# Attention with beacons and a two-layer MLP on one core: the first eight head pairs put in another order

## The chip, the cores and the metric

The kernel runs on one core of one Trainium2 chip. The metric is the time of one execution on the device in microseconds (us), the median over runs. Each core has five engines that run side by side, each with its own queue of instructions: PE (matrix multiply; PEld is its weight load), DVE (vector), ACT (scalar functions), POOL and SP. They wait for each other by semaphores. DMA transfers are issued from the queues of SP, ACT and POOL and move over 16 shared DMA engines.

## What is computed

Causal attention for B = 8 batches, H = 8 heads, S = 576 rows of D = 64, with Nb = 16 "beacon" keys and values that every row sees, and then a two-layer MLP without gate on the 4608 rows of 512:

```python
k_all = np.concatenate([beacon_k, k], axis=2)
v_all = np.concatenate([beacon_v, v], axis=2)
scores = scale * np.matmul(q, k_all.transpose(0, 1, 3, 2))
scores = np.where(causal, -1000000000.0, scores)      # beacons are never masked
a = np.exp(scores - scores.max(-1, keepdims=True))
a /= a.sum(-1, keepdims=True) + 1e-09
x = np.matmul(a, v_all)                               # -> [4608, 512]
h = x @ w_in                                          # [512, 2048]
out = np.maximum(0.01 * h, h) @ w_out                 # [2048, 512]
```

Inputs and output are fp32; the kernel multiplies in bf16 and sums in fp32.

## The kernel before, in words

**Pairs.** Two heads make a pair; pair g = 4 x batch + head pair, 32 in all. Scores are kept transposed (keys on partitions), so that the exponentials are the weights of the second product.

- `score(g, n)` (L286), four parts n = 0..3 of a pair: matmuls of K against Q into one of two PSUM buffers "sc" (L297), then an exp on ACT into the buffer aT (L306). Part n+2 can only start when the exp of part n has freed its buffer. The scores' maximum is not subtracted.
- `masks(g)` (L310): four affine selects on POOL (L320) put zeros where the diagonal blocks are masked.
- `value(g, half)` (L332): aT against V with a column of ones, so the row sums come along (L351); DVE takes the reciprocal (L360) and multiplies (L361) into x_nat. Half 0 has 12 matmuls, half 1 has 18.
- `finish(g)` (L526) calls `x_transposes(g)` (L368): five transposes on PE, one copy on DVE into xT (L378), the MLP's input.

**Q and K.** DMAs issued by POOL bring them in as bf16, two heads of q or k each (L135). For batches 0 and 1, `t_q(g, which)` (L228) transposes them on PE (36 small matmuls a pair, L247) and copies them from PSUM on DVE or ACT (L250); the 16 beacon columns of K are copied on DVE (L238). For batches 2 to 7 POOL permutes them (`permute`, L164), a transposing DMA issued by SP turns them (`turn_pairs`, L262), and POOL puts them in order (`in_order`, L269: L275, L277). K has two buffers (L98), Q two, the raw loads three. The first pair's q and k come in as fp32 by SP and ACT (L152) and are cast on DVE and ACT (L471, L472).

**V** comes in as fp32 by SP (`load_v`, L206), six DMAs a batch, and POOL casts it (`cast_v`, L224), five casts a batch.

**The MLP** works in chunks of 512 rows, 9 in all. Its unit is a *group* of four matmuls of 128x512: `moe1` (L382) makes one of 16 column blocks of the first layer (L387) with the leaky ReLU on ACT (L394); `moe2` (L398) does a quarter of one of four output tiles of the second (L409), after four of which DVE copies the tile (L418) and SP stores it (L420). `fill()` (L425) puts the next group into PE's stream, first and second layer in turn where both can run. A chunk's first layer can start when `finish` has made its rows. There are 288 groups.

**Order.** The order of each engine's queue is written out by hand. Pairs 0 to 7 are in L538 to L562, with three groups among pairs 6 and 7; then a block of its own (L564 to L588) ends pairs 5 to 7 and does 27 more groups before pair 8's first score, so that 30 are done there. From pair 8 on, the groups are spread evenly over eight slots of each pair (L591 to L626). POOL's queue holds in one line all of this: the loads of q, k, w_in and w_out (`loads`, L482), the casts of V, the masks, the permutes and the putting in order. A load issued by POOL waits until the eighth load before it in that queue has landed, as one semaphore serves every eighth.

34 dummy matmuls on the identity stand at the start (`warm_up`, L440).

## Time and profile before

| what | value |
|---|---|
| median of 7 runs | 356.78 us (355.19 to 358.25) |
| time of the profiled execution | 356.68 us |
| span of the profiled execution | 354.9 us |
| PE busy | 340.9 us (96%) |
| POOL busy | 202.0 us (57%) |
| ACT busy | 189.2 us (53%) |
| DVE busy | 94.5 us (27%) |
| first-layer matmuls (L387) | 576, 140.2 us |
| second-layer matmuls (L409) | 592, 139.6 us |
| DMA moved | 40.87 MB, mean 115 GB/s |

The span runs from the first to the last recorded instruction, the time also holds what lies around it. Busy times of an engine count overlapping matmuls once. The profile has a page with the span in 40 slices (a digit is a busy share in tenths), groups of instructions by line, and the chain of work that ended last; the trace gives a time line, with what ended each wait in brackets, and busy times by stretch.

### The profile page before, as it was taken

How to read it: one execution, taken by the hardware profiler on the slowest of the kernel's cores; microseconds unless marked ns; L12 is line 12 of the kernel's file. 1: busy time of each engine (PE TensorE's matmuls, PEld its weight loads, DVE VectorE, ACT ScalarE, POOL GpSimd, SP SyncE). 2: the span in 40 equal slices, each digit the busy share in tenths (PEclk: the TensorE clock that was granted, in tenths of full speed). 3: DMA queues.
4: the chain of work that ended last, by engine and by line, in shares of the span. 5: the costliest groups of instructions: out<-in, count | busy, mean ns of one | idle time of the engine just before them, and what ended most of it. 6: DMA issues, size and time to landing. Idle time of an engine off the chain costs nothing.

```text
span 354.9 us, 7340 instructions
## 1 busy us (share of the span) xinstructions
PE 340.9 (96%) x3002; PEld 172.8 (49%) x3002; DVE 94.5 (27%) x231; ACT 189.2 (53%) x278; POOL 202.0 (57%) x343
## 2 busy tenths in 40 slices
PE   5888999999899999999999999999999999999996
PEld 5566554444454444444444445444444554444444
DVE  2387530102233223221232223222222241000111
ACT  3959754476455873378337843686358403633300
POOL 7599927399899899957695769574441100000000
PEclk9579999999999999999999999999999999999999
DMA  8999999997796986992589355900110011000012
GB/s 163 205 204 167 196 202 195 222 201 128 168 193 118 171 149 120 151 218 36 97 148 223 57 98 119 172 2 1 61 59 2 0 62 59 2 30 30 31 59 88
DMA packets 86929, 40.87 MB, mean 115 GB/s; under 512 B 69872, under 2 KB 82160, under 8 KB 86896
## 3 DMA queue, kind: packets, MB, share of 16 engines
q1 hardware_dynamic: 73456, 26.75, 34.8%
q0 software_dynamic: 13152, 13.34, 24.5%
q10 hardware_dynamic: 288, 0.33, 0.4%
q8 instruction: 23, 0.38, 0.4%
q14 instruction: 10, 0.08, 0.1%
HBM read 37.22 MB, written 9.44 MB: 131 GB/s over the span
## 4 chain that ended last, share of the span: by engine, by line
PE 75%; DMA 9%; POOL 8%; DVE 3%; ACT 2%; issue 2%; SPq 1%; POOLq 0%; ACTq 0%
PE acc L409 32%; PE acc L387 27%; PE sc L297 7%; PE av L351 7%; DMA w_out_sb<-in_moe_w_out_dram 4%; DMA q_raw<-in_q_dram 2%; POOL aT L320 2%; PE tp L373 2%; DMA v_raw<-in_v_dram 1%; DMA v_raw<-in_k_dram 1%; POOL kT L277 1%; POOL qT L277 1%; ACT aT L306 1%; DVE osb L418 1%; PE tp L247 1%
## 5 line engine op out<-in xcount | busy, mean ns | idle before, releaser
L387 PE MATMUL acc<-xT,w_in_sb 128*128 128x512 bf16 x576 | 140.2, 379 | 1.4 <-DVE xT L378 1.4
L409 PE MATMUL acc<-w_out_sb,gT 128*128 128x512 bf16 (+1 forms) x592 | 139.6, 373 | 0.0
L306 ACT ACTIVATE aT<-sc 128x1024 bf16<-128x1024 f32 (+3 forms) x128 | 104.3, 869 | 64.7 <-PE sc L297 64.5
L394 ACT ACTIVATE gT<-acc 128x512 bf16<-128x512 f32 x144 | 85.9, 601 | 79.2 <-PE acc L387 79.2
L409 PEld LDWEIGHTS <-gT 128*128 128x128 bf16 x592 | 53.3, 98 | 58.7 <-issue 6.1
L320 POOL TENSOR_SCALAR_AFFINE_SELECT aT<-aT 128x384 bf16<-128x384 bf16 (+2 forms) x128 | 52.6, 450 | 50.1 <-PE av L351 40.2
L387 PEld LDWEIGHTS <-w_in_sb 128*128 128x128 bf16 x576 | 51.9, 98 | 59.5 <-issue 4.2
L418 DVE COPY osb<-acc 128x512 f32<-128x512 f32 (+1 forms) x37 | 25.1, 677 | 134.7 <-PE acc L409 134.6
L351 PEld LDWEIGHTS <-aT 128*128 128x128 bf16 (+1 forms) x960 | 37.5, 99 | 14.7 <-issue 2.8
L297 PE MATMUL sc<-qT,kT 64*128 64x80 bf16 (+4 forms) x384 | 37.0, 296 | 5.2 <-ACT aT L306 1.6
L351 PE MATMUL av<-v_aug,aT 128*128 128x65 bf16 (+1 forms) x960 | 40.7, 196 | 0.0
L361 DVE TENSOR_TENSOR x_nat<-av,rec 128x384 bf16<-128x384 f32 x64 | 31.4, 491 | 2.2
L224 POOL CAST v_aug<-v_raw 128x512 bf16<-128x512 f32 (+1 forms) x40 | 23.2, 620 | 9.6 <-DMA v_raw<-in_v_dram 9.6
L277 POOL COPY qT<-q_turn 128x576 bf16<-128x576 bf16 x24 | 28.2, 1174 | 0.0
L277 POOL COPY kT<-k_turn 128x576 bf16<-128x576 bf16 x24 | 28.0, 1168 | 0.0
L378 DVE COPY xT<-tp 128x576 bf16<-128x576 bf16 x32 | 14.5, 454 | 49.8 <-PE tp L373 49.8
L297 PEld LDWEIGHTS <-kT 64*128 64x128 bf16 x384 | 12.7, 96 | 30.7 <-issue 18.2
L360 DVE RECIPROCAL rec<-av 128x6 f32<-128x6 f32 x64 | 11.9, 187 | 58.7 <-PE av L351 58.7
L135 POOL DMA_DIRECT2D k_raw<-in_k_dram x31 | 19.3, 624 | 4.2 <-DMA w_out_sb<-in_moe_w_out_dram 4.2
L135 POOL DMA_DIRECT2D q_raw<-in_q_dram x31 | 19.0, 613 | 2.9 <-DMA w_out_sb<-in_moe_w_out_dram 2.8
L164 POOL COPY q_nat<-q_raw 128x1152 bf16<-128x1152 bf16 x12 | 13.8, 1147 | 5.9 <-DMA q_raw<-in_q_dram 5.9
L373 PEld LDWEIGHTS <-x_nat 128*128 128x128 bf16 (+2 forms) x160 | 11.2, 98 | 9.6 <-DVE x_nat L361 1.9
(36 smaller groups left out, 87.6 us busy)
## 6 DMA issues: line engine op xcount, KB each, us to landing
out_dram<-osb SPq DMA_DIRECT2D x35, 256.0 KB, 2.2
v_raw<-in_v_dram SPq DMA_DIRECT2D x24, 256.0 KB, 5.2
q_raw<-in_q_dram POOLq DMA_DIRECT2D x31, 144.0 KB, 4.7
k_raw<-in_k_dram POOLq DMA_DIRECT2D x31, 144.0 KB, 5.2
w_in_sb<-in_moe_w_in_dram POOLq DMA_DIRECT2D x4, 512.0 KB, 6.8
w_out_sb<-in_moe_w_out_dram POOLq DMA_DIRECT2D x4, 512.0 KB, 12.9
v_raw<-in_v_dram SPq DMA_DIRECT2D x8, 224.0 KB, 3.8
v_raw<-in_v_dram SPq DMA_DIRECT2D x8, 160.0 KB, 5.1
```

The costliest lines, as they stand in the source:

```text
L135: dma = nc.gpsimd.dma_start(out=dst[e * RP : (e + 1) * RP], in_=src[b, h0 : h0 + 2].rearrange("h (p i) d -> p h i d", i=RI),)
L224: eng.tensor_copy(out=dst[0 : ROWS[c], c, :, 0:D], in_=t[0 : ROWS[c], c])
L277: nc.gpsimd.tensor_copy(out=dst.rearrange("c (p i) -> c p i", i=RI), in_=t[:, :, e].rearrange("c i p -> c p i"),)
L297: nc.tensor.matmul(out=sc[:, par, col - c0 : col - c0 + w], lhsT=kT[ps_, c * 128 : (c + 1) * 128], rhs=qT[ps_, q0 : q0 + w], start=True, s ...
L306: nc.scalar.activation(out=aT[:, :, c0 : c0 + w], in_=sc[:, :, 0:w], func=AF.Exp, scale=0.125)
L320: nc.gpsimd.affine_select(out=part, in_=part, compare_op=ALU.is_ge, fill=0.0, base=base, channel_multiplier=-1, pattern=pattern,)
L351: nc.tensor.matmul(out=avv[:, n, 0 : D + 1], lhsT=aT[0 : ROWS[c], par, a0 : a0 + 128], rhs=va[0 : ROWS[c], c, 2 * hp + par, :], start=(c = ...
L361: nc.vector.tensor_tensor(out=x_nat[:, t0:t1].rearrange("p t e d -> p (t e) d"), in0=avv[:, :, 0:D], in1=rec[:, n0:n1, None].to_broadcast( ...
L387: nc.tensor.matmul(out=acc, lhsT=w_in_sb[:, j, fc * 128 : (fc + 1) * 128], rhs=xT[:, j, i * 512 : (i + 1) * 512], start=(j == 0), stop=(j ...
L394: nc.scalar.activation(out=gT[i][:, fc, :], in_=acc, func=AF.Prelu, alpha=0.01)
L409: nc.tensor.matmul(out=acc[:, 0:w], lhsT=gT[i][:, fc, t * 128 : (t + 1) * 128], rhs=w_out_sb[:, fc, c0 : c0 + w], start=(fc == 0), stop=(f ...
L418: nc.vector.tensor_copy(out=osb[:, 0:w], in_=acc[:, 0:w])
```

## The change

What it does, by place:

- **Start.** The beacons of batches 0 and 1 are loaded first (by ACT); those of batches 2 to 7 move from the start to pair 7, on POOL. 24 dummy matmuls, the two batches' beacon transposes, 18 dummies, then the transposes of pair 0's Q and K with 4 and 3 dummies behind them. The cast of the first k is split over ACT and DVE, and the copy of the first K into two halves.
- **K has three buffers.** The beacon columns of pairs 2 to 7 are written by POOL, some pairs ahead; all copies of K from PSUM but the first are on DVE.
- **Pairs 0 and 1** have 14 dummy matmuls each among their scores, and their masks are three multiplications by a triangle of ones on DVE (`masks_by_tri`) instead of selects on POOL.
- **Loads.** w_in and w_out come in two halves each instead of four quarters. The first half of w_in is issued during pair 1, behind the Q and K of pairs 4 and 5 and ahead of those of pairs 6 and 7; its second half and w_out's first during pair 6, w_out's second after the masks of pair 7.
- **Pairs 6 and 7.** Eight groups stand at and in pair 6 and five in pair 7, where pairs 5 to 7 are also finished; 17 more follow before pair 8. The second layer starts after 26 first-layer groups instead of 16.
- **From pair 8 on**, POOL puts Q and K in order two pairs ahead (behind the scores of a pair) instead of one; pairs 8 and 9 are done before the cast of batch 2's V; Q and K of batch 3 are loaded before it too; the permutes and loads of the next batch stand behind a pair's masks.

The diff, cut to its core:

```diff
-    k_bufs = [singles.tile([128, NKB * 128], BF16, name=f"kT{i}") for i in range(2)]
+    k_bufs = [singles.tile([128, NKB * 128], BF16, name=f"kT{i}") for i in range(3)]
...
+    def load_w_in(half):
+        cols = slice(half * DF // 2, (half + 1) * DF // 2)
+        return nc.gpsimd.dma_start(out=w_in_sb[:, :, cols], in_=w_in_r[:, :, cols])
+
+    def load_w_out(half):
+        rows = slice(half * NF // 2, (half + 1) * NF // 2)
+        return nc.gpsimd.dma_start(out=w_out_sb[:, rows, :], in_=w_out_r[:, rows, :])
...
-        load_beacon_k(0, 1, nc.scalar)
+        load_beacon_k(0, 2, nc.scalar)
...
+    def beacon_columns(g, eng):
+        b, hp = divmod(g, NPAIR)
+        eng.tensor_copy(out=k_bufs[g % 3][:, 0:NB], in_=bkT[:, b, hp])
...
+        parts = 2 if g == 0 and which == 1 else 1
+        for part in range(parts):
+            p = slice(part * RP // parts, (part + 1) * RP // parts)
+            copy(
+                out=dst.rearrange("c (p i) -> c p i", i=RI)[:, p],
+                in_=ps[:, 0:S].rearrange("c (i p) -> c p i", i=RI)[:, p],
+            )
...
+    def make_tri():
+
+        nc.gpsimd.memset(tri, 1.0)
+        nc.gpsimd.affine_select(
...
+    def masks_by_tri(g):
+
+        aT = probs[g]
+        diag = aT[:, :, 512 : 512 + 3 * 464].rearrange("p e (c x) -> p e c x", c=3)[:, :, :, 0:128]
+        for part, seen in (
+            (aT[:, :, 0:112], tri[:, None, NB:128].to_broadcast([128, 2, 112])),
+            (diag, tri[:, None, None, :].to_broadcast([128, 2, 3, 128])),
+            (aT[0:80, :, 1648:1728], tri[0:80, None, 0:80].to_broadcast([80, 2, 80])),
+        ):
+            nc.vector.tensor_tensor(out=part, in0=part, in1=seen, op=ALU.mult)
...
-        can2 = i2 < NCH and i2 < i1
+        can2 = i2 < NCH and i2 < i1 and done1[0] >= NF + 10
...
+    def keep_busy(n):
+
+        if not busy:
+            busy.append(ps_one.tile([128, 512], FP32, name="av", tag="one"))
         for i in range(n):
-            nc.tensor.matmul(out=ps[:, 0:128], lhsT=ident, rhs=ident, start=True, stop=True)
+            nc.tensor.matmul(out=busy[0][:, 0:128], lhsT=ident, rhs=ident, start=True, stop=True)
...
-        load_beacon_k(1, B, nc.sync)
         load_v(0, after=first)
         load_v(1)
         make_pads()
+        cast_beacon_k(0, 2, nc.scalar.copy)
+        keep_busy(24)
+        beacon_transposes(0, 2)
+        beacon_columns(0, nc.vector)
+        beacon_columns(1, nc.vector)
+        nc.vector.tensor_copy(out=first_cast[0], in_=first_raw[0])
+        nc.scalar.copy(out=first_cast[1][:, 0], in_=first_raw[1][:, 0])
+        nc.vector.tensor_copy(out=first_cast[1][:, 1], in_=first_raw[1][:, 1])
+        keep_busy(18)
+        t_q(0, 0)
+        keep_busy(4)
+        t_q(0, 1, nc.scalar.copy)
+        keep_busy(3)
+        make_tri()
         make_ones()
...
+        beacon_columns(2, nc.gpsimd)
+        cast_v(0, nc.gpsimd, 0, 2)
+        load_qk(1, 0, (0,))
 
         def loads(g):
             b, hp = divmod(g, NPAIR)
             if g == 1:
-                cast_v(0, nc.gpsimd, 3, 5)
+                beacon_columns(3, nc.gpsimd)
+                cast_v(0, nc.gpsimd, 2, 5)
+                load_qk(1, 0, (1,))
+                load_w_in(0)
             elif g == 2:
-                load_qk(1, 1)
+                beacon_columns(4, nc.gpsimd)
             elif g == 3:
-                cast_v(1, nc.gpsimd, 0, 3)
-                load_w_in(0)
+                load_qk(1, 1, (0,))
+                beacon_columns(5, nc.gpsimd)
             elif g == 4:
-                cast_v(1, nc.gpsimd, 3, 5)
-                load_w_in(1)
-                load_w_in(2)
+                load_qk(1, 1, (1,))
+                beacon_columns(6, nc.gpsimd)
             elif g == 5:
-                load_w_in(3)
-                load_w_out(0)
-                load_w_out(1)
...
+                beacon_columns(7, nc.gpsimd)
+            elif g > 2 * NPAIR and b < B - 1:
+                if hp == 0:
+                    load_v(b + 1)
+                    load_qk(b + 1, 0)
+                elif hp > 1:
+                    turn_pairs(b + 1, hp - 2)
...
+            if g < 6:
 
                 score(g, 0)
                 score(g, 1)
...
+                if g < 5:
+                    t_q(g + 1, 0)
+                    t_q(g + 1, 1)
+                    if g in (1, 2):
+                        masks_by_tri(g - 1)
+                if g >= 3:
+                    value(g - 2, 0)
+                if g < 2:
+                    keep_busy(3)
+                score(g, 2)
+                if g < 2:
+                    keep_busy(7)
+                score(g, 3)
+                if g < 2:
+                    keep_busy(4)
+                if g == 2:
+                    value(g - 2, 0)
+                if g >= 2:
+                    value(g - 2, 1)
+                if g >= 3:
+                    finish(g - 3)
+                if g > 1:
+                    masks(g)
+                continue
+
+            if g == 6:
+
+                finish(3)
+                for n in range(4):
                     fill()
+                t_q(6, 0)
+                t_q(6, 1)
+                fill()
+                score(6, 0)
+                score(6, 1)
+                fill()
+                score(6, 2)
+                score(6, 3)
+                cast_v(1, nc.gpsimd, 0, 3)
+                load_w_in(1)
+                cast_v(1, nc.gpsimd, 3, 5)
+                load_w_out(0)
+                masks(6)
+                t_q(7, 0)
+                t_q(7, 1)
+                fill()
+                fill()
+                value(4, 0)
+                value(4, 1)
                 continue
 
+            if g == 7:
+                score(7, 0)
+                score(7, 1)
+                value(5, 0)
+                finish(4)
+                score(7, 2)
+                score(7, 3)
+                masks(7)
+                load_w_out(1)
+                load_beacon_k(2, B, nc.gpsimd)
+                load_qk(2, 0)
+                value(5, 1)
+                value(6, 0)
+                finish(5)
+                value(6, 1)
+                fill()
+                fill()
+                value(7, 0)
+                finish(6)
+                fill()
+                value(7, 1)
+                fill()
+                fill()
+                finish(7)
+                continue
 
+            if g == 8:
                 load_qk(2, 1)
+                cast_beacon_k(2, B, nc.gpsimd.tensor_copy)
                 for grp in range(2):
                     for which in range(2):
                         permute(2, grp, which)
                     turn_pairs(2, grp)
                 load_v(2)
+                while done1[0] + done2[0] < 22:
+                    fill()
+                beacon_transposes(2, B)
+                while done1[0] + done2[0] < 30:
+                    fill()
+                in_order(8)
+                in_order(9)
+                load_qk(3, 0)
                 cast_v(2, nc.gpsimd)
+                load_v(3)
...
             if has(g):
                 score(g, 2)
                 score(g, 3)
+                if has(g + 2):
+                    in_order(g + 2)
...
             if has(g):
                 masks(g)
+                loads_after(g)
```

`loads_after(g)` holds the permutes, the second half of Q and K and the V cast for the next batch that stood in `loads` before. The new dummies' tile takes one of the four PSUM buffers that transposes, values and groups share.

## Prediction

> **What bounds the kernel now.** I read the 40 slices first, then the busy times by stage, the time line, and the chain of waits.
>
> ```profile
> PE   5888999999899999999999999999999999999996
> PEclk9579999999999999999999999999999999999999
> DMA  8999999997796986992589355900110011000012
> ```
>
> PE is full from the fourth slice to the end; losses can only lie in the first 100 us or so. The tail is untouched by the change. Steady state: one chunk's groups and four pairs take 37.32 us (a first-layer run starts at 188.29 and the next at 225.61). A group of four matmuls takes 0.863 us (12 in 2.59), 32 make 27.6, so a pair costs PE (37.32-27.6)/4 = 2.42 us. Pairs 0 to 7 also have Q and K transposed on PE, 0.76 each (27.16 to 27.92).
>
> Up to pair 8 PE should need 8x2.42 + 7x0.76 + 8 groups (6.9) = 31.6 us from the first score (8.55) to the last transpose of pair 7 (49.66), which is 41.1: 9.5 us lost. From there 22 groups run without a gap (19.0) to the first score of pair 8 at **68.59**, with 30 groups done. What follows loses some 2 us: 351.43-68.59 = 282.8 against 24x2.42 + 258x0.863 = 280.7.
>
> ```profile
> 8.00:9.00 1.00, 0.45 (x4) 0.11 (x4) 0.00 (x0) 0.51 (x2) 0.76 (x1) 1.00 1.22 203
> 9.00:10.00 1.00, 1.00 (x37) 0.93 (x36) 0.20 (x1) 1.00 (x2) 0.00 (x0) 0.53 1.19 198
> ...
> 21.00:22.00 1.00, 1.00 (x8) 0.32 (x5) 0.67 (x3) 0.53 (x1) 1.00 (x4) 0.50 1.35 218
> ```
>
> Columns: stretch, length, PE, PEld, DVE, ACT, POOL busy, granted clock, DMA, GB/s. PE idles most of 5 to 9 us, then the clock is half until 22 us. Four score matmuls took 0.58 us at 8.55 and 1.11 at 11.66. DMA moves about 200 GB/s all the while.
>
> ```profile
> 23.63 1.38 DVE L238 COPY kT<-bkT 128x16 bf16<-128x16 bf16 x1
> ...
> 96.80 0.58 PE L297 MATMUL sc<-qT,kT 64*128 64x512 bf16 x4 [1.12 <-POOL kT L277]
> ```
>
> The first is a 16-column copy, 0.16 alone, that takes 1.38 beside POOL's masks (23.61 to 25.25) and holds K of the next pair. In the second PE waits for POOL's copy of K. The chain of waits comes to it through these pieces:
>
> ```profile
> 37.11 13.01 DMA w_out_sb<-in_moe_w_out_dram
> 50.41 7.33 DMA q_raw<-in_q_dram
> ```
>
> POOL's loads of batch 2 wait for w_out: that chain must not get longer.
>
> **Part by part.** I follow the start of each pair's exps on ACT: before, 8.98, 12.30, 15.94, 21.47, 26.21, about 29.9 (pairs 0 to 5). A pair's four exps take 1.86+1.41 = 3.27. Its scores come in four parts with two PSUM buffers, so part three waits for the first exp, part four for the second.
>
> *Start.* K of pair 0 lands at 6.12 and is cast in 1.15 on ACT; now ACT and DVE take a half each (0.6, an estimate). The copy into K (0.64) is halved, and the first two scores need only the first half (0.4). K transposes 0.47, score to exp 0.45. So 6.14+0.6+0.05+0.55+0.45+0.45 = about 8.3: 0.7 earlier. The two batches of beacons that ACT's queue now loads (64 KB for 32) cost little; 224 KB leave SP's queue, about 1 us of DMA at 200 GB/s, which brings V of batch 0 that much earlier.
>
> *Fillers and clock.* 24 dummy matmuls replace 34, 25 more stand around the transposes, 14 each in pairs 0 and 1. One is 0.112 (34 in 3.81); at twice the clock I estimate 0.056. 14 make 0.8 or 1.6 us. At full clock the scores of a pair take 1.1 (0.58 and 0.48, at 25.72 and 28.32) and transposes 0.76, so that PE has 1.4 to spare of 3.27, and the fillers lie beside ACT and cost nothing; the cover gone, they cost the 0.8. I take full clock: PE idle led to half clock here, and the fillers fill it. Then pairs 0 and 1 take 3.3 each: 8.3, 11.6, 14.9.
> The Trainium skill's "TensorE: Matmul & The Clock Gate" (Part 1) has a window of about 3.4 us of activity deciding the clock, and its Part 4 says transposes do not count as busy in the same way; the row from 9 to 22 us, busy with transposes at half clock, does not contradict it. By that rule the fillers would have to carry the clock, and by it the time is that of rival 2, 357.2, unless their 0.8 us in 3.3 is enough.
>
> *Masks of pairs 0 and 1 on DVE.* Three multiplies over 224, 768 and 160 columns. From the normalizing rows (557 ns for 384, 424 for 256: 1.04 ns a column and 0.16 fixed) 1.7 us at most; at three of the smallest copies 0.5 at least. I take 1.7, the nearer row. DVE then has 1.5 (two copies) + 1.35 (normalizing) + 1.7 in pair 2, over the 3.3: 0.5 us late for pair 4's Q and K, hidden under the wait below.
> The skill's "GPSIMD Engine Reference" (1. Specifications) says VectorE instructions with two SBUF inputs contend with POOL, which is casting V then; the 1.38 us copy above is such a contention. By it each multiply may wait up to 1.2 us, and pair 2 would end about 1 us later.
>
> *V of batch 0.* Its last piece landed at 17.85 (12.25+5.6); 1 us less traffic makes it 16.9, cast by 17.5. PE wants it at 14.9+2.55: nearly no wait. Pair 3: 18.4 (3.45 from exp to exp, by PE's order: part four starts 2.0 in and takes 0.15, the second half of a value 0.55 (41.26 to 41.81), five transposes 0.3, the next score 0.45).
>
> *Q and K of batch 1, first w_in half.* The first two loads leave POOL after two casts, about 14.2 to 15.4; before, a like load landed 5.3 to 6.0 after its issue. K lands at 20.0, PE wants it at 19.0. Behind that wait stand a value and parts three and four on PE, and ACT waits for those: a pair of 4.25. Pair 4: 22.65. The other two leave at 17.5 to 18.7, land at 24.1, wanted at 23.3: 4.05. Pair 5: **26.7**, 3.2 ahead of before. w_in's half is issued at 18.7. Bytes by then to land: 0.65 MB first pair and beacons, 0.88 Q/K, 2.36 V of two batches, 0.59, 1.05: 5.5 MB, which before had moved by 29.6. It is wanted at 30.5: hidden, by about 1 us. What hides it is pairs 2 to 5. Bounds: nothing, or, with the landing of the slowest w_out (14.8), 33.5 and 3.0 of cost, all of PE's queue standing behind it. I take nothing, as the one w_in issued at 26.82 beside V loads took 5.5.
>
> *Pairs 6 and 7 with 13 groups.* Pair 3's transposes need the normalizing at 26.7+3.5 = 30.2. Then on PE: 0.3, 4 groups 3.45, Q/K 0.76, group 0.86 (34.7 to 35.55); K's copies on DVE (0.76+0.75) end at 36.05, a wait of 0.5; two scores, a group, and the fourth score must wait for the second exp until 38.55 (1.1 lost). Q/K of pair 7, 2 groups, value 4: 42.15. In pair 7 only 0.65 us of work lies under two exps: 1.3 lost, 44.7. Values 5 to 7 with masks, 5 groups and four transposes: 52.6. The second w_in half, issued about 34, has till 47. 17 more groups (14.7) and 0.4 for the beacons: pair 8 at **67.7**, by PE. Gain 0.9.
>
> *Batch 2 on POOL.* Here w_out's second half is issued after pair 7's masks: 47.8 (exps end 46.2, masks 1.6), where before all of w_out was out at 38.6. Each issue on POOL waits for the landing of the eighth before it, so the last two Q/K loads of batch 2 wait for w_out and the beacons; behind them in POOL's queue stand the permutes, on which SP's transposes wait, and the copies for pairs 8 and 9. A 512 KB load took 5.5 us on a short queue, 2.6 of it data: 1 MB takes 8.1, to 55.9. 2.43 MB from 47.8 at 200 GB/s plus 2.9: all landed at 62.9. Two permutes 2.3, 65.2, then pair 8's copies 2.4: 67.6. It ties with PE's 67.7: no loss, no reserve.
>
> *Two pairs ahead.* A third K buffer lets POOL's copies run two pairs ahead and before the V cast. Counting POOL's queue on from 67.6 (copies of pair 9 to 70.1, loads 72.6, cast to 76, pair 10 to 78.5, masks 80.1, pair 11 to 82.6) each stands 2 to 5 us before its score. The waits of 0.41 at 88.96 and 1.12 at 96.80 go: 1.5. What is late next is PE itself. Bounds: nothing, or the whole 2.
>
> *Small moves.* The beacon columns of pairs 2 to 7 (0.2 each) go from DVE to POOL, out of reach of the 1.38 us stall, ahead of each pair's masks (1.62); with two loads (1.2) POOL has 3.0 of 3.4. ACT loses two K copies (0.65), DVE gains them (0.75), already counted in its 3.3. Making the triangle adds 0.5 to POOL at 5 us, where it sat idle for 4.27. The second layer starts after 26 groups instead of 16, at 52.6+13x0.863 = 63.8; both halves of w_out are there by 55.9. On SP, V of batches 2 and 3 (12 loads, some 11 us from 66.7) now stand together ahead of the first output store; with a second-layer tile finished only every 7 to 9 us and three output buffers, nothing waits.
>
> **Sum:** 0.9+1.5 = 2.4 off the profiled execution's 356.68 (span 354.9 and 1.8 around it): **354.3**. Its time is 0.1 under the median 356.78, so the forecast is the same for the median, 0.7% faster.
>
> **Rivals.**
> 1. *Nothing waits for DMA.* Pair 5 at 8.3+2x3.3+3x3.45 = 25.25, pair 8 at 66.25: gain 2.3+1.5, 352.9 (352.4 with the whole 2). For it: bigger rows in w_in. Against: DMA full throughout, and batch 2 must be 1.4 us earlier too.
> 2. *It doesn't do what it says: the clock stays at half.* Pairs 0 and 1 then take 1.9+1.1+1.6 = 4.6, pair 2 5.0: pair 3 at 22.5; the Q/K waits vanish, pair 5 at 29.6, pair 8 at 70.6: 2.0 lost, 1.5 won: 357.2. For it: PE was 0.8 to 1.0 busy from 9 to 22 us and stayed at half. Against: fillers are dense.
> 3. *Slower: w_out's second half holds batch 2's Q and K.* Place: POOL between pair 7's masks and pair 8's copies. At w_out's median landing (12.9) it lands at 60.7, the loads at 67.7, pair 8 at 72.4: 3.8-1.5 = 2.3 lost, 359.0. It decides from pair 8 at 67.7, breaks even at 70.1, and is slower by 0.5% (1.8 us) from 71.9. For it: the chain of waits runs there already. Against: those 12.9 us were behind three other weight loads.
>
> **Numbers.** Forecast 0.43, rivals 0.17, 0.15, 0.25. 0.5% is about what a measurement of this kernel tells from no change (355.0 and 358.6). Faster: 0.32 of the forecast and rival 1: 0.49. Same: the forecast's remaining 0.11 and 0.12 of rival 2: 0.23. Slower 0.28: rival 3, and 0.03 of rival 2 with a wait added. The range takes rival 1 with its bound and rival 3: 352.0 to 359.0.
>
> **What would show it.** Right: clock above 0.9 from 9 to 22 us; first exp at 8.3; pair 5's near 26.7; groups from 30.5 without a wait for w_in; pair 8's score near 67.7; no wait for POOL's K copy from 85 to 100 us. Wrong: the clock at half; a PE wait for Q and K of batch 1 above 1.5 us, or for w_in; pair 8 waiting for POOL.

## The result and the profile after

The changed kernel takes **361.14 us** (median of 12 runs, 357.84 to 362.52) against 356.61 of the kernel before (31 runs on the same chip): ratio 1.0112, 95% interval 1.0089 to 1.0135. It is 1.1% slower where 0.7% faster was forecast. The profiled execution took 362.03 us, its span is 360.3. The medians here and below are of all runs, while the ratios leave out a run that is over 1.5% above the fastest of its kernel (two of `w_out_early`, one each of `three_links` and `two_links_hold_regroup`), so a ratio isn't always the quotient of two medians.

The 40 slices of the changed kernel, the same three lines as of before:

```profile
PE   7978989998989999999999999999999999999996
...
PEclk9999999999989999999999999999999999999999
DMA  8996969996869689775916695463110011000012
```

A slice is 9 us. The digits 5 and 7 at the start of the clock line have become 9: the clock stays up there. PE has holes in the third and fourth, the sixth, the tenth and the twelfth slice (18 to 36, 45 to 54, 81 to 90 and 99 to 108 us). Of these the sixth, tenth and twelfth are new, while the hole that before had in its eleventh slice is gone. The clock has a dent in the twelfth.

The time line of PE at the places where the span was lost; in brackets the wait ahead of the line and what ended it:

```profile
23.91 0.47 PE L253 MATMUL tp<-ident,q_raw 64*64 64x64 bf16 x18 [1.23 <-DMA q_raw<-in_q_dram]
24.62 0.47 PE L253 MATMUL tp<-ident,k_raw 64*64 64x64 bf16 x18 [0.24 <-DMA k_raw<-in_k_dram]
...
70.11 0.59 PE L306 MATMUL sc<-qT,kT 64*128 64x512 bf16 x4 [0.38 <-POOL kT L286]
...
84.22 0.59 PE L306 MATMUL sc<-qT,kT 64*128 64x512 bf16 x4 [1.41 <-POOL kT L286]
...
100.81 0.99 PE L306 MATMUL sc<-qT,kT 64*128 64x512 bf16 x4 [2.62 <-POOL kT L286]
...
115.99 0.59 PE L306 MATMUL sc<-qT,kT 64*128 64x512 bf16 x4 [0.39 <-POOL kT L286]
```

The first two lines are the transposes of pair 5, the others the first scores of pairs 8, 10, 12 and 14. The waits for POOL's copies of K come to 4.80 us, where the kernel before had 1.5. Pair 12's four matmuls take 0.99 instead of 0.59: they run at half clock. Stretches of 1 us show how a wait turns into half clock at pair 5 (stretch, length, PE, PEld, DVE, ACT, POOL busy, granted clock, DMA, GB/s):

```profile
23.00:24.00 1.00, 0.09 (x6) 0.09 (x8) 0.00 (x0) 1.00 (x2) 1.00 (x4) 1.00 1.12 208
24.00:25.00 1.00, 0.76 (x36) 0.63 (x36) 0.58 (x1) 0.38 (x1) 1.00 (x4) 1.00 1.13 205
25.00:26.00 1.00, 1.00 (x24) 0.77 (x20) 0.99 (x3) 0.00 (x0) 0.14 (x1) 0.69 1.14 212
26.00:27.00 1.00, 1.00 (x21) 0.78 (x17) 0.56 (x1) 0.84 (x2) 0.00 (x0) 0.50 1.12 198
```

PE is idle in 23 to 24, works again from 24, and only then, at 25.4, the clock halves, until 28.8 by the same stretches: the price is paid on work that had already got its data.

POOL's time line in the changed kernel carries the rest:

```profile
48.95 0.90 POOL L114 DMA_DIRECT2D w_out_sb<-in_moe_w_out_dram  x1
...
58.47 0.60 POOL L133 DMA_DIRECT2D q_raw<-in_q_dram  x1 [4.21 <-DMA w_out_sb<-in_moe_w_out_dram]
60.05 0.59 POOL L133 DMA_DIRECT2D k_raw<-in_k_dram  x1 [0.98 <-DMA bk_raw<-in_beacon_k_dram]
...
67.78 1.16 POOL L286 COPY qT<-q_turn 128x576 bf16<-128x576 bf16 x1 [1.22 <-DMA q_turn<-q_nat]
68.88 1.17 POOL L286 COPY kT<-k_turn 128x576 bf16<-128x576 bf16 x1
...
78.45 0.62 POOL L227 CAST v_aug<-v_raw 128x512 bf16<-128x512 f32 x1 [2.02 <-DMA v_raw<-in_v_dram]
81.23 0.61 POOL L227 CAST v_aug<-v_raw 80x512 bf16<-80x512 f32 x1 [2.17 <-DMA v_raw<-in_v_dram]
...
89.60 1.14 POOL L167 COPY q_nat<-q_raw 128x1152 bf16<-128x1152 bf16 x1
...
91.78 0.61 POOL L133 DMA_DIRECT2D q_raw<-in_q_dram  x1
...
99.61 1.15 POOL L286 COPY kT<-k_turn 128x576 bf16<-128x576 bf16 x1 [4.15 <-DMA k_turn<-k_nat]
```

Read it from the top: the second half of w_out is issued at 48.95 and holds the last load of batch 2's Q until 58.47; the load of the beacons, issued right behind it, holds the last of K until 60.05. Permutes, the transposing DMA and the copies for pair 8 follow and end at 70.05, and PE has waited 0.38 us for them when it starts at 70.11. Nothing on POOL is ahead of PE from there. The casts of batch 2's V then wait another 4.19 us in front of pair 10's copies, and the copy for pair 12 waits 4.15 us for a transposed K that was permuted at 90.68 and sent at 92.15, beside four loads issued at 91.78 to 94.2.

The same transposing DMA of K for pair 12 in the time lines of the kernel before (SP's, then the copy on POOL that reads it) and of the changed kernel (SP's):

```profile
82.97 1.60 SPq L262 DMA_TRANSPOSE k_turn<-k_nat  x1
...
95.59 1.15 POOL L277 COPY kT<-k_turn 128x576 bf16<-128x576 bf16 x1
```

```profile
92.15 1.63 SPq L271 DMA_TRANSPOSE k_turn<-k_nat  x1
```

From issue to landing it took 7.2 us before and 7.4 in the changed kernel, both times beside four loads (before, from 82.59). So it didn't become slower. What shrank is the room it has: before, POOL came to the copy 12.6 us after the issue; now it comes 3.3 us after it, at 95.46. The copy runs a pair earlier and the permute half a pair later.

The same stations stand in the chain of waits of the changed kernel (start, length, what):

```profile
49.84 9.92 DMA bk_raw<-in_beacon_k_dram
62.64 5.09 DMA q_turn<-q_nat
...
71.41 6.99 DMA v_raw<-in_v_dram
...
95.46 4.14 issue
```

From 48.2 to 116.0 this chain holds no work of PE, only POOL's and what POOL waits for: POOL's queue sets the pace there. The last piece shown is called "issue", but POOL's own line, at 99.61, names the DMA.

**Where the loss sits.** I split each profiled span at the first score of pair 8; what follows it is the same work in all kernels.

| kernel | pair 8's first score | from there to the end of the span |
|---|---|---|
| before | 68.6 | 286.3 |
| forecast (354.3 - 1.8 = 352.5 in all) | 67.7 | 284.8 |
| changed | 70.1 | 290.2 |
| `w_out_early` | 68.2 | 288.4 |
| `batch3_behind_cast` | 67.4 | 288.2 |
| `permute_early` | 68.8 | 287.6 |
| `two_links` | 69.0 | 284.2 |
| `two_links_regroup` | 67.1 | 284.1 |

Of 7.8 us between the forecast and the profiled span, 2.4 came before pair 8 and 5.4 after it. Each row is one execution; the profiled ones lie up to 2.7 us off the median of their kernel, so small differences between rows mean little.

### The profile page after: what moved, and what is told of

It reads as the page before. It is cut to its first block, busy times and chain, and to the rows that moved or that the text cites. A ratio compares the mean times of both kernels' runs of the same rounds, so it can differ in the third digit from the quotient of the medians.

```text
span 360.3 us, 7392 instructions
## 1 busy us (share of the span) xinstructions
PE 342.7 (95%) x3045; PEld 173.3 (48%) x3045; DVE 95.3 (26%) x235; ACT 187.7 (52%) x277; POOL 199.1 (55%) x340
## 3 DMA queue, kind: packets, MB, share of 16 engines
q0 software_dynamic: 12128, 13.54, 24.6%
## 4 chain that ended last, share of the span: by engine, by line
PE 69%; DMA 11%; POOL 10%; issue 4%; DVE 2%; SPq 2%; ACT 1%; POOLq 0%; ACTq 0%
PE acc L422 28%; PE acc L444 28%; PE av L386 6%; PE sc L306 5%; DMA v_raw<-in_v_dram 3%; DMA bk_raw<-in_beacon_k_dram 3%; DMA k_raw<-in_k_dram 2%; POOL aT L355 2%; POOL qT L286 2%; DMA q_turn<-q_nat 1%; DMA v_raw<-in_k_dram 1%; POOL v_aug L227 1%; PE tp L408 1%; POOL kT L286 1%; SPq L218 1%
## 5 line engine op out<-in xcount | busy, mean ns | idle before, releaser
L422 PE MATMUL acc<-xT,w_in_sb 128*128 128x512 bf16 x576 | 138.8, 379 | 1.4 <-DVE xT L413 1.4
L355 POOL TENSOR_SCALAR_AFFINE_SELECT aT<-aT 128x224 bf16<-128x224 bf16 (+1 forms) x120 | 48.4, 437 | 27.6 <-ACT aT L315 15.1
L408 PE MATMUL tp<-ident,x_nat 128*128 128x128 bf16 (+2 forms) x160 | 14.2, 219 | 0.5 <-DVE x_nat L396 0.5
```

What stands on the lines that cost most here:

```text
L355: nc.gpsimd.affine_select(out=part, in_=part, compare_op=ALU.is_ge, fill=0.0, base=base, channel_multiplier=-1, pattern=pattern,)
L408: nc.tensor.transpose(ps[:, q0 : q0 + rows], x_nat[0:rows, t].rearrange("p e d -> p (e d)"), ident[0:rows, 0:rows],)
L422: nc.tensor.matmul(out=acc, lhsT=w_in_sb[:, j, fc * 128 : (fc + 1) * 128], rhs=xT[:, j, i * 512 : (i + 1) * 512], start=(j == 0), stop=(j ...
```

## The experiments

Ratios are against the kernel before, run on the same chip (its median was 356.3 to 356.6 us each time). **Theory one:** w_in's half, ahead of Q and K of pairs 6 and 7 in POOL's queue, takes the DMA from batch 1. **Theory two:** w_out's second half holds batch 2's Q and K on POOL. After the first four runs, theory two became a theory of two links, with the order of batch 3's permutes as the second. All edits are made on the changed kernel.

**w_in_later: 359.52 us (4 runs), ratio 1.0108 (1.0071 to 1.0146).**

```diff
             if g == 1:
...
                 load_qk(1, 0, (1,))
-                load_w_in(0)
...
             elif g == 3:
+                load_w_in(0)
                 load_qk(1, 1, (0,))
```

> The first half of w_in is issued two pairs later, behind the masks of pair 2 and just ahead of the Q and K of pairs 6 and 7 (about 20.5 us instead of 18.0). Theory one (front): in the changed kernel PE waits at 23.9 us for Q and K of pair 5 because that 1 MB takes half of the DMA while they land, and the idle time makes the clock fall to half until 28.5 us. Then the wait of 1.47 us and the stretch at half clock go, pair 5's first exp comes at about 26.9 instead of 28.5, and the time falls by 1.5 us, to about 359.6; w_in, landed at about 26 before, still lands before 32. Theory two (back): only what holds POOL's copies of K from 70 us on counts, so that PE catches up early and waits longer later: no change, 361.

By the ratio the loss stayed; the median is 1.6 us lower, where theory one put it, but four runs don't part the two. In the profiled run, the longest of the four, PE waited just as long one pair earlier with w_in out of the way: 1.06 and 0.90 us at the transposes of pair 4. The clock fell for longer:

```profile
20.00:25.00 5.00, 4.10 (x89) 2.87 (x85) 3.15 (x7) 2.35 (x4) 4.16 (x10) 0.76 1.29 210
25.00:30.00 5.00, 5.00 (x91) 3.64 (x85) 3.05 (x7) 3.12 (x5) 3.19 (x9) 0.55 1.14 209
```

Pair 5's first score came at 28.81, later than in the changed kernel (27.82). The waits at pair 4 aren't w_in's, which was issued only at 20.52: Q and K of pair 4 went out 1.3 us later than in the changed kernel (14.59 for 13.29), as POOL's cast ahead of them had waited 1.35 us for V. For pair 5 the test is weak: its K landed 6.8 us after its issue instead of 7.1. So w_in's place alone doesn't make batch 1 late; that it adds something isn't ruled out.

**w_out_early: 356.58 us (10 runs), ratio 1.0004 (0.9972 to 1.0036).**

```diff
                 load_w_out(0)
+                load_w_out(1)
                 masks(6)
...
                 masks(7)
-                load_w_out(1)
```

> The second half of w_out is issued right behind the first, during pair 6 (about 37 us instead of 49). Theory two (back): in the changed kernel the four waits of PE for POOL's copies of K (0.38, 1.41, 2.62, 0.39 us, and 3 us at half clock behind the third) come from w_out's second half, for which the last loads of batch 2's Q and K wait (4.21 us on POOL at 58 us, 0.98 for the beacons). Then the permutes of batch 2 start some 5 us earlier, the waits go, and the time falls by 4 to 5 us, to about 356.5. Rival: these waits come from POOL's later order (loads of batch 3 ahead of batch 2's V cast, permutes behind the masks); then only the 0.38 goes, and the time stays at 360.5 or above.

The median falls by 4.6 us, and the kernel is level with before. The last two Q/K loads of batch 2 are out at 54.12 and 56.05 instead of 58.47 and 60.05. PE's time line in `w_out_early`, first scores of pairs 8, 10 and 12:

```profile
68.18 0.59 PE L306 MATMUL sc<-qT,kT 64*128 64x512 bf16 x4
...
80.82 0.59 PE L306 MATMUL sc<-qT,kT 64*128 64x512 bf16 x4
...
97.08 0.58 PE L306 MATMUL sc<-qT,kT 64*128 64x512 bf16 x4 [2.29 <-POOL kT L286]
```

The waits before pairs 8 and 10 are gone, pair 12's is not, though POOL came to it 3.7 us earlier (90.42 for 94.12). So something else is late there: since the change the permutes of batch 3 stand behind the masks of pair 9 (85.89 to 88.1), K's transposing DMA goes out at 88.45, and the copy waits 4.10 us for it. Before the change the permutes were at 80.41.

**batch3_behind_cast: 359.12 us (6 runs), ratio 1.0086 (1.0051 to 1.012).**

```diff
                 in_order(9)
-                load_qk(3, 0)
                 cast_v(2, nc.gpsimd)
-                load_v(3)
+                load_qk(3, 0)
...
+            elif g == 9:
+                load_v(3)
```

> The loads of batch 3's Q and K stand behind the cast of batch 2's V on POOL, and batch 3's V is loaded one pair later, so that batch 2's V does not share the DMA with them. Rival of theory two: the V cast's waits (2.02 and 2.17 us at 78 and 81 us) go, POOL's copies for pair 10 come some 4 us earlier, PE's waits of 1.41 and 2.62 us go as well, and the time falls by 3 to 4 us, to about 357.5. Theory two: the chain is late from the start and these only pass it on; the 1.41 goes (1 to 1.5 us, 359.8), the 2.62 stays, since the permutes of batch 3 now wait for loads that are issued later.

The median is 2.0 us lower, but the interval of the ratio overlaps the changed kernel's (1.0089 to 1.0135), so the gain in time isn't shown. What it acts on is. With no load of batch 3 beside it, V of batch 2 is cast by 75.4 instead of 81.8, and pair 10 has no wait. Pairs 8, 12 and 14 still wait 0.32, 1.96 and 1.82. So the loads beside batch 2's V act on pair 10, as w_out's place does, and not on pair 12.

**no_fillers: 360.47 us (4 runs), ratio 1.012 (1.0082 to 1.0158).** The 28 dummy matmuls of pairs 0 and 1 are left out.

```diff
-                if g < 2:
-                    keep_busy(3)
                 score(g, 2)
-                if g < 2:
-                    keep_busy(7)
                 score(g, 3)
-                if g < 2:
-                    keep_busy(4)
```

> The 28 dummy matmuls among the scores of pairs 0 and 1 are left out; the 49 at the start stay. If they hold the clock, it falls to half between 10 and 22 us, pair 3's first exp comes at 20.5 to 21.5 instead of 18.0, and the time rises by up to 2 us (the front is not the only bound): 361 to 363. If the start alone holds it, pair 3 starts at 18.0 and the time is the same, 361.

```profile
10.00:15.00 5.00, 3.21 (x56) 1.68 (x55) 2.73 (x6) 4.85 (x8) 2.91 (x6) 0.84 1.15 201
15.00:20.00 5.00, 5.00 (x86) 3.40 (x86) 3.60 (x9) 3.59 (x5) 4.60 (x10) 0.50 1.17 220
```

Without them PE is busy 3.21 of 5 us, the clock halves at 13.4 (0.70 in 13 to 14), and pair 3's first exp comes at 19.57 instead of 18.02. So in this run nothing but the dummies is missing, and the clock falls. The total of four runs doesn't show it: pair 5 has to wait for its Q and K anyway, and the 1.5 us are spent there (its first score came at 27.14, in the changed kernel at 27.82).

**permute_early: 357.56 us (10 runs), ratio 1.0031 (1.0001 to 1.006).** Only the first two permutes of the next batch go back ahead of the scores; w_out stays where the change put it.

```diff
+                elif hp == 1:
+                    for which in range(2):
+                        permute(b + 1, 0, which)
                 elif hp > 1:
                     turn_pairs(b + 1, hp - 2)
...
-                if hp in (1, 2):
+                if hp == 2:
                     for which in range(2):
-                        permute(b + 1, hp - 1, which)
+                        permute(b + 1, 1, which)
```

> On the changed kernel, only the two permutes of the next batch's first four heads go back ahead of a pair's scores (half a pair earlier on POOL); w_out's second half stays behind pair 7's masks. Theory of two links (w_out's second half holds batch 2's Q and K; batch 3's transposed K is late because its permute was put behind masks and beside the next loads): the second link alone goes: the wait of PE for POOL's K before pair 12 falls from 2.62 us to below 0.5 and the half clock behind it with it, while the waits before pairs 8 and 10 (0.38 and 1.41) stay; 361.1 - 2.6 = 358.5 us. Rival (the transposing DMA is slow whenever it is issued, since loads run beside it): a wait of 2 us or more before pair 12 stays, 361 us.

The median falls by 3.6 us. Pairs 8 to 14, even ones, in PE's time line of `permute_early`:

```profile
68.76 0.58 PE L306 MATMUL sc<-qT,kT 64*128 64x512 bf16 x4 [0.26 <-POOL kT L286]
...
83.50 0.59 PE L306 MATMUL sc<-qT,kT 64*128 64x512 bf16 x4 [2.03 <-POOL kT L286]
...
97.39 0.59 PE L306 MATMUL sc<-qT,kT 64*128 64x512 bf16 x4
...
112.04 0.58 PE L306 MATMUL sc<-qT,kT 64*128 64x512 bf16 x4 [1.29 <-POOL kT L286]
```

Pair 12's wait and its half clock are gone, pairs 8 and 10 still wait: two links, each with its own place. The rival falls with it: K's transposing DMA, issued at 87.50 with the next loads 3.6 us behind it, took 4.2 us, and its copy came 7.2 us after the issue. A wait of 1.29 before pair 14 had been hidden behind pair 12's.

**two_links: 354.82 us (10 runs), ratio 0.9956 (0.9927 to 0.9984).** Both of these edits.

> Both links undone: w_out's second half right behind its first in pair 6, and the first permutes of the next batch ahead of the scores. Theory of two links: w_out early alone gave 356.6 us and kept a wait of 2.29 us before pair 12; that goes, pair 12's first score comes 26.7 us after pair 8's instead of 28.9, 356.6 - 2.3 = 354.3 us. Rival (POOL has no room: what is moved forward delays the copies for pair 11): a wait of 1 to 2 us stands before pair 11 or 14 instead, 356 us.

No first score waits for POOL any more. PE's time line in `two_links`, pairs 8 and 12:

```profile
69.00 0.58 PE L306 MATMUL sc<-qT,kT 64*128 64x512 bf16 x4
...
95.53 0.59 PE L306 MATMUL sc<-qT,kT 64*128 64x512 bf16 x4
```

26.5 us lie between them, where the changed kernel had 30.7. The kernel is faster than before the change by 0.4%, and pair 12's K, copied on POOL at 90.68 to 91.91, stands 3.6 us before its score. The rest of the span, 284.2 us, is all but PE's own time: 281.1 us to its last matmul, where the prediction's sum has 280.7, and 3.1 us behind that.

**three_links: 354.23 us (10 runs), ratio 0.9952 (0.9922 to 0.9981).** The edit of `batch3_behind_cast` besides (batch 3's V loaded in pair 9, ahead of the permutes).

> As before, and batch 2's V cast ahead of batch 3's loads, with batch 3's V loaded one pair later. Theory: POOL's waits for V of batch 2 (2.64 and 2.46 us with w_out early) shrink to below 1 us each, but there is no PE wait left that they cause, so the time is that of the two links undone, 354.3 us. Rival: batch 3's Q and K, issued some 7 us later, are late for their permutes and pair 12 waits again for 1 to 2 us, 355.8 us.

No further gain that the intervals could tell: as expected, POOL's waits for V had no PE wait behind them any more. The rival's wait before pair 12 didn't come.

**three_links_qk_first: 355.39 us (7 runs), ratio 0.9946 (0.9912 to 0.998).** Q and K of pair 5 are loaded right behind those of pair 4.

```diff
         cast_v(0, nc.gpsimd, 0, 2)
-        load_qk(1, 0, (0,))
+        load_qk(1, 0)
...
                 cast_v(0, nc.gpsimd, 2, 5)
-                load_qk(1, 0, (1,))
                 load_w_in(0)
```

> As before, and Q and K of pair 5 issued right behind those of pair 4, ahead of the last three casts of batch 0's V (2.4 us earlier). Theory that the front's loss is the wait for Q and K of pair 5 and the fall of the clock behind it: PE's wait at that transpose falls from 1.23 and 0.24 us to below 0.3 together, the clock in 20 to 30 us stays above 0.9, pair 5's first score comes at 25.5 instead of 27.8 in the changed kernel, and the time is 1 to 2 us under the kernel without this move, 352.8 us. Rival (the landing is set by the bytes ahead in the 16 engines, V of batch 0 and 1 among them, not by the issue): the wait stays above 0.8 us, or V's casts come late by as much, and the time is the same, 354.3 us.

No gain, and neither theory was quite right. The wait for Q and K did go, but for 0.41 us at pair 4's K. But V's last three casts, now behind these two loads, came to lie beside the masks on DVE. DVE's and PE's time lines in `three_links_qk_first`:

```profile
16.58 3.42 DVE L343 TENSOR_TENSOR aT<-aT,tri 128x224 bf16<-128x224 bf16 x3
```

```profile
20.75 0.54 PE L386 MATMUL av<-v_aug,aT 128*128 128x65 bf16 x12 [1.15 <-DVE x_nat L396]
```

The three multiplies of one pair, 1.04 us in the changed kernel, take 3.42 us beside POOL's casts (15.63 to 17.40) and selects (from 18.22). They delay the normalizing, PE waits 1.15 us for that, and the clock falls all the same (0.70 in 20 to 25 us, 0.62 in 25 to 30). This is the contention that the prediction drew from the Trainium skill's "GPSIMD Engine Reference" (1. Specifications): the changed kernel's own profile shows almost none, this run shows it at 2.4 us, and `three_links` and `w_in_later` at 0.9 and 1.0 (1.90 and 2.04 us). The 1.38 us copy that the prediction put under the same rule has one input, not two; that it waited for the same reason isn't shown.

**hold_clock: 360.80 us (6 runs), ratio 1.0122 (1.0091 to 1.0152).** On the changed kernel, dummies where PE waits for Q and K of pairs 4 and 5.

```diff
+                    if g > 2:
+                        busy[:] = []
+                        keep_busy(10)
                     t_q(g + 1, 0)
+                    if g > 2:
+                        keep_busy(4)
                     t_q(g + 1, 1)
```

> On the changed kernel, 10 dummy matmuls ahead of Q's transposes and 4 ahead of K's of pairs 4 and 5 (0.056 us each, 0.78 us a pair). Theory: where PE waits for Q and K of these pairs the dummies lie in the wait; the waits come from DMA and stay, but the clock no longer falls behind them: granted clock 1.00 from 20 to 30 us instead of 0.66, pair 5's first score 1.0 us earlier (26.8 instead of 27.8), 360.1 us. Rival (the fall of the clock costs nothing, the waits alone do): the clock stays up, pair 5's first score stays within 0.3 of 27.8 and the time is 361.1 us, or up to 1.5 us more where the dummies stand in the way.

**two_links_hold: 355.53 us (12 runs), ratio 0.9979 (0.9963 to 0.9996).** The same dummies on `two_links`.

> The same dummies on the kernel with both links undone. Theory: clock 1.00 from 20 to 30 us, pair 8's first score at 68.0 instead of 69.0, nothing that waits for POOL behind it, 354.8 - 1.0 = 353.8 us. Rival (clock costs nothing, dummies stand in the way): 354.8 to 356.3 us.

Neither wins anything: `hold_clock` has the ratio of the changed kernel, `two_links_hold` is no faster than `two_links`. Both profiles show the clock at 1.00 in every stretch from 13 to 30 us, but in `hold_clock` it then fell at 30.8, after PE had waited twice for exps. Pair 5's first score comes at 28.47 and 27.86, in `two_links` at 27.17 in spite of half clock. From pair 4's first score to it, it takes 5.29 and 5.03 us with the dummies, 5.17 in `two_links` with the fall, and 3.98 in `w_out_early`, which had neither. So the dummies cost about what the fall does. The runs, sorted by their mean clock, say the same of the dummies:

| kernel, mean us of | runs with a mean clock of 0.999 or more | the others |
|---|---|---|
| before | 356.5 (22 runs) | 356.5 (45) |
| changed | 358.9 (4) | 361.6 (8) |
| `two_links` | 353.7 (4) | 355.6 (6) |
| `two_links_hold` | 355.2 (8) | 356.4 (4) |

In the three later kernels a run in which the clock falls somewhere is 1.2 to 2.7 us longer. That isn't all the clock's price, since it falls behind waits that cost time themselves, and in the kernel before the runs with a fall are not longer. Among runs at full clock the dummies cost 1.5 us. Whether they make such runs more frequent is open: 8 of 12 instead of 4 of 10, but 1 of 6 in `hold_clock` instead of 4 of 12.

**two_links_regroup: 355.63 us (12 runs), ratio 0.9956 (0.9927 to 0.9984).** Pair 6's Q and K are transposed ahead of its first groups, and PE work stands between the last two score parts of pairs 6 and 7.

```diff
-                for n in range(4):
-                    fill()
                 t_q(6, 0)
                 t_q(6, 1)
-                fill()
+                for n in range(4):
+                    fill()
...
                 score(6, 2)
+                fill()
                 score(6, 3)
...
                 score(7, 2)
+                value(5, 1)
                 score(7, 3)
...
-                value(5, 1)
                 value(6, 0)
```

> Both links undone, and in pairs 6 and 7 the pieces of PE work put between the waits: Q and K of pair 6 are transposed ahead of its first four groups, one group stands between parts three and four of pair 6, and a half of pair 5's values between parts three and four of pair 7. Theory: the waits of 0.36 (DVE's copy of K) and twice 0.48 us (exps) go, 1.3 us together: pair 8's first score 1.3 us earlier from the same pair 5, 354.8 - 1.3 = 353.5 us. Rival (POOL's chain to pair 8's K becomes the bound, as w_out's landing is not moved): a wait for POOL of about as much before pair 8, 354.8 us.

**two_links_hold_regroup: 353.46 us (7 runs), ratio 0.9928 (0.9899 to 0.9957).** Both on `two_links`.

> Both of these on the kernel with both links undone. Theory: the gains add, 354.8 - 1.0 - 1.3 = 352.5 us. Rival: POOL's chain is the bound before pair 8 (a wait for K's copy of 1 us or more there), 354 us.

In the profile of `two_links_regroup` the 0.36 and both waits of 0.48 are gone, and from pair 5's first score to pair 8's it takes 40.7 us, in `w_out_early`, `two_links` and `two_links_hold` 41.6 to 41.8: a gain of 0.9 to 1.1 of the 1.3 expected; the transposes of pair 6, now earlier, wait 0.43 for their K. In the medians it doesn't show by itself (the same ratio as `two_links`); with the dummies the version is the best of this study, 0.7% under the kernel before, though the intervals don't part it from `two_links`. Its profiled run is the longest of its seven (360.28 us) and shows a limit of the dummies: K of pair 0 came late, PE waited 1.21 us for it, the clock fell at 8.9, and it stayed at half until 19.1, although the 28 dummies of pairs 0 and 1 ran and PE was busy from 9 us on.

## Why the prediction was wrong

**Right.**
- *Start:* pair 0's first exp at 8.16 (8.3 forecast, 8.98 before).
- *Clock and dummies:* 1.00 until 25 us, so rival 2 is out; the exps of pairs 0 to 2 follow each other without a gap from 8.16 to 17.56. Pair 3 came at 18.02 (18.4 forecast), pair 4 at 22.52 (22.65).
- *Masks on DVE:* 0.88 and 1.04 us, less than the 1.7 taken.
- *w_in:* the first group started at 32.25 with no wait for it, 1.7 after the forecast because pair 5 was late. That was luck in part: the load landed 12.5 us after its issue, at 30.5, just when the forecast wanted it and not 1 us ahead.
- *Work behind pair 8:* with the POOL waits undone it took 284.2, as the sum had it with the whole 2 us won (284.8 with 1.5).

One reading of the slices was off, without effect on the sum: PE is full from the fifth slice on, not the fourth, and the eleventh has a hole, where the two waits for POOL are.

**Wrong, in order of weight.**

1. *"Each stands 2 to 5 us before its score"* (two pairs ahead) is the step that failed. It counted POOL's own instructions from 67.6 and none of their waits. The V casts were to end at 76 and ended at 81.8: V of batch 2 is issued by SP only behind the four transposing DMAs, from 69.08, and shares the DMA with batch 3's loads, put ahead of the casts by the same change. And batch 3's permutes, whose move the prediction named in the change, got no place in the count at all: they run on POOL and feed a DMA on SP which a copy on POOL waits for, so half a pair later there, and the copy a pair earlier, left that DMA 3.3 us of room, of the 12.6 it had; it needs 7.4, and that came out as 4.15 us of wait at 99.61. It forecast a gain of 1.5 and there was a loss of 3.9 (290.2 against 286.3); `w_out_early`, `permute_early` and `two_links` show it: 288.4, 287.6 and 284.2.

2. *"It ties with PE's 67.7: no loss, no reserve"* (batch 2 on POOL). The order was right, two terms were short. w_out's half was issued at 48.95, not 47.8, and let the load behind it go at 58.47, 9.5 us later, where 8.1 was taken; so the permutes of the last loads began at 64.18, not 62.9. And between permute and copy stands the transposing DMA, which had no term and cost 1.22. POOL ended pair 8's copies at 70.05 instead of 67.6. This is rival 3's mechanism, with chance 0.25. Its time of 359.0 is nearer to the result than the forecast, but its account isn't the run's: it put pair 8 at 72.4 with the gain behind it kept, where pair 8 came at 70.1 and the delay was paid at pairs 10, 12 and 14. A tie with no reserve should have been carried on into the next step, not left at zero.

3. *Pair 5 at 26.7* came at 28.53. K was to land at 24.1, 0.8 after PE wanted it, and landed at 24.57, 7.12 after its issue where 5.3 to 6.0 had been read; PE waited 1.47. What the step lacked is what a wait of that size does to the clock: half clock from 25.4 to 28.8. Pairs 4 and 5 of `w_out_early`, the same code up to 37 us, waited 0.32 and 0.67 and kept the clock. There pair 5's K was transposed 0.29 earlier (24.33 for 24.62) and its first score came 1.25 earlier (26.57 for 27.82), so 1.0 of pair 5's delay of 1.8 us is the clock's. The term varies from run to run, as the table of runs above shows.

On the clock, the Trainium skill's "TensorE: Matmul & The Clock Gate" (Part 1) has an activity window of about 3.4 us that is free-running, so that the point of a transition varies from run to run; it says this of the start of a kernel. The rows here agree in that a stretch at half clock lasted 3.4 us, and in that busy time alone doesn't tell whether the clock falls. From 21 to 25 us PE was busy 2.30 of the 4 us in the changed kernel and 2.92 in `two_links`, and the clock fell in both; it was busy 2.59 in `w_out_early`, and there it didn't fall. Where the window began no run here shows.

The range, 352.0 to 359.0, ended at rival 3. It left out that the gain of the "two pairs ahead" step could turn into a loss by the same mechanism; 359.0 with the 1.5 lost and another 2 us added would have held the result.

**Open:** why Q and K of batch 1 land earlier or later in the same code (pair 4's K 4.1 us after its issue at 13.88 in the changed kernel, 5.9 after 13.84 in `two_links`). Moving w_in didn't settle it, and loading them earlier ran into DVE's contention.

## What to carry to other kernels

When work is moved to run further ahead, count the whole loop, DMAs and the queues that issue them included, from the moved load to the engine that needs it: here a K passes POOL's queue three times (load, permute, copy), with a DMA behind the first two. Moving one end forward and the other back takes the room away twice from what lies between. A step that comes out as a tie is a risk for every step behind it, and gets its loss in the sum. Two delays on one chain can hide parts of each other and must be undone together: behind pair 8 of the profiles they gave back 1.8 and 2.6 us singly, 6.0 together. In the medians of whole runs it was 4.6, 3.6 and 6.3, with the front's chance falls of the clock in them; either alone left the kernel no faster than before, both made it faster.

## What the runs showed of the hardware

- Waits of 1.23 and 0.24 us on PE, the last ended at 24.6, were followed by half clock from 25.4 to 28.8, when work had come back; against `w_out_early` that cost another 1.0 us. In `w_in_later` it was half from 22.6 to 29.5 with PE busy throughout.
- With 14 dummy matmuls a pair (0.8 us in 3.3) the clock stayed at full speed through pairs 0 and 1; without them it fell at 13.4 (`no_fillers`). They don't bring it back: in `two_links_hold_regroup` it stayed at half from 8.9 to 19.1 beside them.
- Three multiplies on DVE, 0.88 us alone, took 3.42 beside POOL's casts and selects.
- The transposing DMA of K for pair 12, with four loads issued beside it, took 7.2 us before the change and 7.4 after; issued 3.6 us ahead of these loads it took 4.2 in `permute_early` and 4.7 in `two_links`.
